# A third written order for 4871 operations of one attention and MLP kernel

## The chip, the cores and the metric

The kernel runs on one core of a Trainium2 chip, as one program. Its time is the device time in microseconds (us), the median of three runs. Besides the times there is one profiled execution of the kernel before, taken by the hardware profiler, with every instruction's start and duration. The engines are named as the profile names them: PE is TensorE, DVE is VectorE, ACT is ScalarE, POOL is GpSimd, and SP is the engine that issues most of the DMAs.

## The reference

```
scale = 1 / sqrt(64);  q, k, v: (8 batches, 8 heads, 576, 64), q and k drawn 8 times larger than v
k_p, v_p = k, v averaged over groups of 8 positions          # 576 -> 72 keys
scores = scale * q @ k_p^T;  scores -= max(scores)
attn = exp(scores) / (sum(exp(scores)) + 1e-09)
x = (attn @ v_p), heads side by side                        # (4608 tokens, 512)
h = x @ w_in                                                # 512 -> 2048
g = h * 1 / (1 + exp(-1.702 * h))
out = g @ w_out                                             # 2048 -> 512, float32
```

## The kernel before

**Attention.** Each of the eight batches goes through the same steps. Two heads' keys at a time are put on the partitions; scores go to PSUM tiles `sps` (L1148, PE), DVE takes the row maximum `nm` from each (L1171) and subtracts it into `sc` (L1179), ACT takes the exponential (L1200), DVE the sum (L1205). The weights are then copied into `main` and `tail` (L1271, L1262), turned by DVE (`mt`, L1378; `tt`, L1320) and cut into a high and a low part (`ah`, `al`, L1385, L1389; `at`, L1341, L1344). PE multiplies them with the values into `pav` (L1406 to L1409). Three instructions read each `pav`: `x` (L1448, its high part), `xt` (L1460, a copy) and the low part (L1451, always DVE). The `sps` and `pav` tiles share two PSUM banks, so a `pav` two further on can begin only when the last of the three reads of its bank is done.

**The MLP.** The tokens go through it in nine chunks: chunks 0 to 7 are the first 512 tokens of each batch, chunk 8 the 8 times 64 left over. Chunks 0 and 1 multiply in the plain way, three matmuls for each product of high and low parts (L1693 to L1695 into `h`, L1735 to L1737 into `o`). While chunk 1 runs, sums of weight blocks are made (`fold`: L1774, L1818, L1756, L1759, L437 and L440) and written to DRAM. Chunks 2 to 8 use a scheme of the Strassen kind with these sums: PE makes products in `ha` and `hb` (L1982), ACT or DVE copies them out (L1997), DVE adds (L2005), ACT takes the activation (L2017), the result is cut in two parts (L437 or L440, L2043, L2048, L2051) and goes into the output products (L2272 to L2274). `ha` and `hb` have two PSUM banks, the outputs four.

**The start.** SP issues loads of raw weights (`raw`, 512 KB each, L1555), of keys and values (`kv`, L622, 256 KB; `tl`, L683) and of queries (L2162). While these are on their way PE does idle matmuls (`warm`, L2225), and the first batch's attention runs before chunk 0.

**What sets the order.** The program first makes 4339 tasks, each with its engine, its instruction and the tiles that it reads and writes. Many tasks can run on a second engine (copies: ACT or DVE; subtractions and sums of SBUF tiles: DVE or POOL). Nothing is sorted when the program is built: the tasks are emitted as the table `ORDER` (L42) lists them, and each engine works off its own instructions in that order. A negative entry means the task's other engine:

```
    with tc.manual_schedule():
        for n in map(int, ORDER.split()):
            t = tasks[n if n >= 0 else -n - 1]
            if n < 0:
                t.swap()
            t.emit()
```

An instruction that waits therefore holds up everything behind it on its engine. Tile names in the lists below carry a batch or half, a piece, and the number of the tile's making.

Of the kernel before, what the change touches and what calls it, by code (L numbers as in the profile page):

```python
# [42 lines left out]
2074 2075 2076 2077 9 155 156 157 10 162 163 164 165 158 2078 2079 2080 2081 2082 73 0 2083 2084 2085 2086 2087 2088  # L43
2089 11 -161 169 170 171 4 6 3 31 1 5 22 159 72 166 172 173 32 25 26 33 7 8 50 2090 2 197 198 45 34 46 167 199 -52 52
23 24 212 47 35 213 36 214 48 49 215 53 21 190 191 192 54 2091 2092 29 12 30 176 177 37 40 41 42 2093 38 39 178 43 44
17 14 13 16 15 18 20 19 183 184 57 55 185 65 200 161 216 168 179 193 186 201 174 68 204 236 220 228 244 417 340 356
348 268 308 260 252 415 284 388 459 292 276 451 175 180 187 181 182 28 56 58 59 60 62 63 64 61 70 67 69 66 -196 -189
74 97 75 76 98 87 102 88 99 205 103 206 100 101 89 82 237 83 -91 207 91 112 104 77 84 189 113 105 -79 106 202 238 194
239 196 208 203 85 92 86 79 107 93 229 230 108 -81 -211 -219 231 81 114 94 117 95 115 109 96 110 111 116 217 221 222
209 223 119 118 120 121 124 123 240 232 2094 2095 2096 2097 2098 2099 2100 2101 2102 2103 219 224 211 226 233 2109  # L50
2110 2111 2112 2113 2114 2115 2116 -2105 136 -138 122 130 245 2117 246 2107 127 128 2105 2106 -132 -2119 247 253 254
261 262 -130 125 126 132 255 456 457 449 2119 133 300 324 416 418 -136 269 263 270 248 227 332 134 -235 235 2108 148
2120 2122 138 249 309 310 149 225 271 -142 -251 311 -140 140 2124 2125 2126 2127 142 2128 2129 2130 2131 277 278 241
-252 279 -144 2132 -2134 -243 -2135 2121 2123 264 256 312 285 286 287 144 150 2135 2137 301 302 27 -148 303 -152 357
145 266 152 146 -154 358 2218 2219 2220 2221 2222 2223 2224 2225 359 257 280 243 267 272 293 294 258 265 419 295 -260
2138 2226 -2228 421 422 -2229 2139 2140 2136 296 2141 2142 2143 2144 2145 2146 2229 2231 2232 282 341 342 343 281 274
349 350 420 -284 351 2147 2148 389 390 448 450 380 452 391 -2150 2233 2234 2235 2236 2237 2238 2239 2240 446 325 326
298 2241 425 426 327 458 154 404 2230 297 460 396 316 317 364 275 -2243 -2244 -300 372 428 427 2150 453 2154 2155 2156
2157 2244 2245 2158 2246 454 2247 304 360 318 273 319 352 288 365 289 366 313 344 320 328 392 429 430 71 424 367 455
333 -315 334 518 467 515 464 433 517 434 516 466 461 -291 462 2159 2160 2161 2162 2163 335 -316 -292 -2165 -307 373  # L60
374 375 519 2151 431 2152 393 305 2248 2249 2250 2251 2252 2253 2153 2254 2255 330 432 329 -308 465 -332 468 463 381
2256 -2258 605 472 604 475 474 525 473 523 524 526 382 322 368 376 336 2165 2166 2169 2170 469 2171 2172 2173 2174
2175 2167 2168 2258 2261 2176 435 346 321 383 345 337 405 361 406 470 476 471 407 423 323 436 347 2177 477 438 439
2178 338 437 -363 527 478 479 353 480 363 339 2259 2184 2185 2186 2187 2188 2189 2263 2190 2191 2260 2264 2265 2266
2267 2268 2269 2270 2262 440 -2180 441 442 2182 2180 481 482 485 484 378 2271 2272 483 354 397 398 -380 -2274 520 521
522 399 2183 528 529 530 2181 539 603 588 533 541 355 2192 540 542 486 589 400 -371 447 532 369 -2194 534 2278 606 444
2276 531 2279 503 2280 2281 -505 487 535 505 445 2194 377 489 490 543 488 371 2199 2200 401 394 2282 2201 491 2277 492
493 506 2197 -508 508 -396 536 537 538 384 385 -387 387 2283 2284 402 2274 544 545 546 494 2275 2285 2195 2286 2287
495 2202 509 -511 496 2203 2204 2196 497 2293 2294 2295 2296 2297 2198 2288 -499 511 499 512 2205 2206 2289 547 -404
2298 2299 2300 408 -411 636 637 639 409 513 2207 2208 411 548 549 514 550 552 551 607 590 2209 500 2291 2292 2308 553  # L70
2290 2214 2215 2309 2310 501 2301 554 613 612 643 592 610 591 2302 556 443 502 557 555 587 2311 2323 2324 558 565 2312
559 566 560 567 2210 2303 2325 2304 593 594 638 568 2326 2327 608 -598 -572 561 -563 640 2313 2314 2315 654 620 611
641 619 651 644 642 2211 -565 569 2316 -2318 412 563 -599 2328 2306 2307 2318 609 570 2329 2330 2342 572 579 -581 2305
2321 2343 2212 2216 573 574 581 2331 595 2332 575 578 600 614 -603 2526 2530 582 583 596 576 601 -600 -2334 577 616
-586 645 2353 2354 584 615 621 2319 2344 2355 2345 413 2320 2356 2322 617 2338 659 2357 2358 2359 414 2339 625 658 624
618 652 656 2546 2334 646 2335 623 2340 2531 2346 2527 2347 657 653 -2551 622 -2538 649 -2539 655 647 660 -2540 2543
648 650 2536 2336 2348 2375 2376 2377 2364 2378 2365 661 2366 2351 2367 2349 2350 2352 634 2551 2547 2368 2548 626 662
2544 2369 2370 -2558 2558 2549 628 664 -2541 -2542 635 728 2542 2559 2566 2545 2363 663 2552 627 665 586 727 2361 629
666 630 2362 -2557 2560 631 667 668 729 730 731 669 -2562 -674 -2571 847 2554 735 -690 2386 2372 2360 2371 2379 2380
685 2563 682 2381 2387 2388 2373 2389 2397 2398 2399 2400 2374 832 744 691 688 2532 675 686 2390 670 2391 2392 2385  # L80
2383 2382 2384 2408 2409 2394 2395 2410 2411 2571 732 -2565 -2554 2565 733 2562 734 -633 -694 2567 2568 2401 692 2528
-2687 -2578 -2579 -678 -685 -2530 -691 -2580 671 2402 2572 676 678 679 680 2687 2688 683 2583 2403 2419 2420 2393 2405
2396 2404 2421 2422 2407 2406 -2577 -2581 -2582 736 674 681 2412 2413 687 -673 -2703 -2534 -2591 2584 2414 -2707 2423
2424 2707 2430 694 697 695 2591 2582 742 2555 831 748 737 740 698 -2587 -2574 2694 696 2690 747 2418 2703 750 749 743
745 2416 2431 2441 2432 2433 706 2417 2415 2585 2425 2597 2587 2704 2434 707 2691 2695 751 746 738 739 741 -2607 -2597
2600 2435 2607 2608 2588 -634 708 -2719 2598 2599 2603 2436 2442 752 753 755 754 756 2428 2429 2426 2443 2444 2439
2427 2437 2452 2453 2440 2438 -2699 -2590 -2611 -2605 -2612 -2617 -2570 -2610 -2690 -2602 757 2605 2602 2612 2445 2446
2447 2617 758 759 760 -762 2696 -2627 2454 2463 2455 2456 2457 2451 2450 2464 2465 2466 2448 2449 2458 2474 2475 2460
2461 2462 699 -2619 -2631 -2620 2699 762 2627 2620 780 2467 -2622 2631 -2638 -775 779 2468 2592 -2723 -2637 -2594
-2639 -2640 768 2692 767 2632 2623 2628 2723 2640 2469 2459 2476 2485 2477 2486 2471 2487 2488 2472 2473 2470 2622  # L90
-2625 -2647 -2642 -2630 2643 -2645 885 700 2647 2478 701 879 2614 2534 2575 2594 2625 881 849 773 2479 2648 2480 713
-2651 2489 2651 2490 -2650 -2715 -2711 -2658 2777 -2634 2750 2642 2645 -2671 -2667 -2614 2654 887 882 -2659 2634 2574
2635 886 2595 2751 2535 2507 2508 2496 2497 709 2481 702 2498 2499 -715 715 -2660 720 -722 -785 722 -2720 -2668 770
771 777 765 781 2715 778 769 763 710 766 775 705 2668 783 785 -704 -713 704 -2670 786 787 -777 -783 711 2491 2693 2483
2484 2482 2509 2510 2492 833 2500 2671 2672 2501 772 2502 716 723 2494 2493 2495 2506 2503 2754 2504 788 726 764 2511
2512 789 2673 796 -798 798 -2677 719 724 2711 717 790 725 718 799 791 2652 2724 801 800 2700 792 793 795 2513 2615 884
2776 2774 2752 880 2753 2775 846 848 2674 2675 835 834 2505 2520 794 -2678 802 -804 804 805 808 810 -812 812 -820 813
2656 2523 2778 2514 2517 823 2755 -817 -821 -822 -828 -829 825 814 2779 -823 2521 829 -827 -825 2783 2757 2784 2515
2791 2792 -2759 2764 830 2796 2765 2798 -818 850 815 851 888 2734 2678 2679 836 2767 2705 2756 2759 806 807 2766 2760
# [2477 lines left out]
```

## Time and profile before

| | |
|---|---|
| median of three runs | 910.27 us (908.38 to 912.41) |
| profiled execution | 908.89 us, span of its instructions 907.0 us |
| PE busy | 855.6 us (94%) |
| DVE busy | 749.7 us (83%) |
| ACT busy | 571.5 us (63%) |
| POOL busy | 321.9 us (35%) |
| mean granted clock of PE | 0.990 |
| chain that ended last | PE 42%, DVE 31%, ACT 12%, DMA 6%, issue 5% |

The span runs from the first to the last instruction; the execution's own time is 1.89 us longer. The chain is followed back from the last instruction, at each step to what released it or to the instruction before it on its engine. Its shares are of the whole span, and stages with different limits are mixed in them. Granted clock is PE's clock as a share of full speed (2.4 GHz); 0.5 is the lower level of 1.2 GHz.

### The profile page before, as it was taken

To read this page: it belongs to the slowest core of one execution; us is meant where nothing else is said; L and a number is where in the kernel's file an instruction comes from. 1 tells how busy PE (TensorE), PEld (TensorE's weight loads), DVE (VectorE), ACT (ScalarE), POOL (GpSimd) and SP (SyncE) were. 2 spreads that over 40 slices of the span, in tenths; PEclk is the share of its full clock that TensorE was granted. 3 is DMA by queue.
4 is the path that set the end of the run, shared out by engine and by line. 5 is a ranking of instruction groups with operands and counts; after the bars stand their busy time and mean duration, and the time that the engine had idled before them with its cause. 6 is when DMAs were issued, how large, how long until landed. Compare 5 with 4: busy or idle time off the path is not lost.

```text
span 907.0 us, 16076 instructions
## 1 busy us (share of the span) xinstructions
PE 855.6 (94%) x5614; PEld 637.9 (70%) x5614; DVE 749.7 (83%) x1571; ACT 571.5 (63%) x1202; POOL 321.9 (35%) x307
## 2 busy tenths in 40 slices
PE   7999999998889888998999899999999999999997
PEld 7879888887666565666666566666667666666885
DVE  6999988879889979998687988999988666555787
ACT  6998853687678777777356645666476654424652
POOL 3765542552226453352332124122142224322122
PEclk9999999999989999999999999999999999999999
DMA  9974303320727653564447333643452155344542
GB/s 286 375 229 125 84 18 97 106 81 31 224 80 210 167 145 87 138 174 115 120 132 200 104 111 95 181 135 96 132 154 89 53 166 181 113 151 137 195 152 59
DMA packets 151313, 125.32 MB, mean 138 GB/s; under 512 B 86336, under 2 KB 108352, under 8 KB 151232
## 3 DMA queue, kind: packets, MB, share of 16 engines
q1 hardware_dynamic: 146384, 115.52, 43.5%
q10 hardware_dynamic: 4848, 8.78, 2.8%
q8 instruction: 44, 0.72, 0.3%
q14 instruction: 37, 0.30, 0.1%
HBM read 102.76 MB, written 21.50 MB: 137 GB/s over the span
## 4 chain that ended last, share of the span: by engine, by line
PE 42%; DVE 31%; ACT 12%; DMA 6%; issue 5%; SPq 3%; POOL 1%; ACTq 0%; DVEq 0%; POOLq 0%
PE ha L1982 9%; PE hb L1982 6%; PE o L2272 4%; PE o L2274 4%; PE o L2273 4%; ACT main L1271 3%; PE sps L1148 2%; ACT slots L2017 2%; DMA raw<-in_moe_w_in_dram 2%; DMA ws<-wd 1%; DVE slots L2005 1%; PE o_P L2502 1%; DVE nm L1171 1%; DVE qt L1132 1%; DVE sc L1179 1%
## 5 line engine op out<-in xcount | busy, mean ns | idle before, releaser
L1982 PEld LDWEIGHTS <-ws 128*128 128x128 f16 x2016 | 195.1, 98 | 81.7 <-issue 24.3
L1982 PE MATMUL ha<-x,ws 128*128 128x256 f16 x1008 | 137.6, 272 | 13.7 <-ACT slots L1997 3.6
L1982 PE MATMUL hb<-x,ws 128*128 128x256 f16 x1008 | 132.4, 273 | 5.5 <-DVE slots L2005 3.7
L2274 PE MATMUL o<-t,glall 128*128 128x512 f16 x256 | 97.0, 379 | 0.1
L2272 PE MATMUL o<-t,ghall 128*128 128x512 f16 x256 | 97.1, 379 | 0.0
L2273 PE MATMUL o<-t,ghall 128*128 128x512 f16 x256 | 97.0, 379 | 0.0
L1997 ACT COPY slots<-ha 128x256 f32<-128x256 f32 x94 | 34.7, 369 | 88.6 <-PE ha L1982 86.4
L2005 DVE TENSOR_TENSOR slots<-slots,hb 128x256 f32<-128x256 f32 x139 | 56.4, 410 | 34.8 <-PE hb L1982 24.3
L2017 ACT ACTIVATE slots<-slots,smalls 128x256 f32<-128x256 f32 (+1 forms) x108 | 61.4, 577 | 34.8 <-DVE slots L2005 33.5
L1693 PE MATMUL h<-x,w 128*128 128x256 f32 (+1 forms) x192 | 63.2, 329 | 1.0 <-ACT g L1710 0.6
L1271 ACT COPY main<-sc 32x384 f32<-32x384 f32 (+2 forms) x117 | 53.0, 453 | 15.5 <-DVE mt L1378 6.1
L1723 POOL TENSOR_TENSOR gl<-g,gh 128x512 fp32r<-128x512 f32 x23 | 31.0, 1347 | 87.0 <-ACT gh L1715 60.8
L1695 PE MATMUL h<-x,w 128*128 128x256 f32 (+1 forms) x192 | 61.2, 319 | 0.0
L1694 PE MATMUL h<-x,w 128*128 128x256 f32 (+1 forms) x192 | 61.1, 318 | 0.0
L2048 POOL TENSOR_TENSOR slots<-slots,smalls 128x512 f32<-128x512 f32 (+1 forms) x32 | 33.6, 1050 | 61.2 <-ACT ghall L437 20.2
L1148 PE MATMUL sps<-k,qt 128*128 128x144 f32 x320 | 49.2, 299 | 5.7 <-DVE sc L1179 2.5
L1389 POOL TENSOR_TENSOR al<-mt,ah 128x256 fp32r<-128x256 f32 (+1 forms) x20 | 17.6, 882 | 98.4 <-ACT ah L1385 39.8
L1148 PEld LDWEIGHTS sps<-k,qt 128*128 128x128 f32 x320 | 44.9, 198 | 9.4 <-issue 3.3
L2274 PE MATMUL o<-t,slots 128*128 128x512 f16 x128 | 48.5, 379 | 1.6 <-DVE slots L2043 1.6
L2272 PE MATMUL o<-t,slots 128*128 128x512 f16 x128 | 48.6, 379 | 0.0
L2273 PE MATMUL o<-t,slots 128*128 128x512 f16 x128 | 48.5, 379 | 0.0
L1982 PE MATMUL ha<-x,shared 128*128 128x256 f16 x336 | 46.3, 275 | 2.3 <-ACT slots L1997 1.1
(399 smaller groups left out, 2269.6 us busy)
## 6 DMA issues: line engine op xcount, KB each, us to landing
ws<-wd SPq DMA_DIRECT2D x168, 256.0 KB
out_dram<-osb ACTq DMA_DIRECT2D x32, 256.0 KB
raw<-in_moe_w_in_dram SPq DMA_DIRECT2D x15, 512.0 KB
raw<-in_moe_w_out_dram SPq DMA_DIRECT2D x15, 512.0 KB
kv_False<-in_k_dram SPq DMA_DIRECT2D x28, 256.0 KB
kv_True<-in_v_dram SPq DMA_DIRECT2D x28, 256.0 KB
shared<-wd SPq DMA_DIRECT2D x56, 128.0 KB
qr<-in_q_dram SPq DMA_DIRECT2D x112, 40.0 KB
```

What stands on the lines that cost most here:

```text
L1148: nc.tensor.matmul(ps()[:, t * PW : (t + 1) * PW], lhsT=qt()[:, s0 : s0 + P], rhs=m.k2()[:, jj], start=True, stop=True,)
L1271: copy(out=main()[32 * r : 32 * (r + 1), :, cols].rearrange("p j t (k a) -> p t j a k", a=2), in_=sc()[rows, ts, :, 16 * r : 16 * (r + 1)] ...
L1693: nc.tensor.matmul(o, lhsT=w[:, 0, j], rhs=xs[:, 0], start=j == 0, stop=False)
L1694: nc.tensor.matmul(o, lhsT=w[:, 1, j], rhs=xs[:, 0], start=False, stop=False)
L1695: nc.tensor.matmul(o, lhsT=w[:, 0, j], rhs=xs[:, 1], start=False, stop=j == NJ - 1)
L1982: nc.tensor.matmul(o, lhsT=wv()[:, r, jj], rhs=xo(k, jj), start=start and n == 0, stop=n == len(terms) - 1,  skip_group_check=not start,)
L1997: t = copy(256, lambda copy: copy(out=part(i), in_=bank()[:, 0:256]), [bank], [at(i)])
L2005: lambda: nc.vector.tensor_tensor(out=part(i), in0=part(i), in1=hb()[:, half * 256 : half * 256 + 256], op=ALU.add),
L2017: lambda: nc.scalar.activation(out=out(), in_=src(), func=AF.Gelu_apprx_sigmoid, scale=inner()),
L2272: nc.tensor.matmul(o(), lhsT=gh()[:, tok], rhs=wp[:, 0], start=start, stop=False)
L2273: nc.tensor.matmul(o(), lhsT=gh()[:, tok], rhs=wp[:, 1], start=False, stop=False)
L2274: nc.tensor.matmul(o(), lhsT=gl()[:, tok], rhs=wp[:, 0], start=False, stop=stop)
```

## The change

Only the table `ORDER` differs: the same 4339 tasks, in another order, and with another choice of engine for some. It has 4871 entries; one stands on average 29 places from where it stood (median 19, at most 373). Negative entries go from 709 to 711. By the lists of instructions, PE has 9177 on both sides and SP 693; DVE has 1571 before and 1555 after, ACT 1174 and 1164 (30 table loads on both), POOL 307 and 334. What moved to POOL is mostly `gl` (L1723, 23 to 29), `al` (L1389, 20 to 23), `at` (L1344, 12 to 16), the low parts L1759 (39 to 41), L2072 (23 to 28), L1818 (10 to 13) and the weighting L1221 (1 to 3). ACT gives and takes L437 (DVE's form is L440: 76 to 65) and L1756 (DVE 13 to 25).

The beginning of the table, before and after:

```diff
 ORDER = """
-2074 2075 2076 2077 9 155 156 157 10 162 163 164 165 158 2078 2079 2080 2081 2082 73 0 2083 2084 2085 2086 2087 2088
...
+2074 72 9 155 156 2075 2076 2077 2078 2079 2080 2081 2082 2083 2084 2085 2 1 157 6 0 5 25 26 23 24 158 160 161 73 3 4
...
```

**DVE at the scores of the third batch's second half**, in the second plain chunk. `sps_1_0` and `sps_1_1` are the first two pieces, in the two banks; `nm` is the maximum and `sc` the subtraction, which frees the bank. Before:

```order
L1171 TENSOR_REDUCE nm_1_2414<-sps_1_1_2410 128x3x2
L1344 TENSOR_TENSOR at_0_1_2392<-tt_0_2390,at_0_1_2392 32x256
L1774 TENSOR_TENSOR stage<-w_6_753 128x512
L1759 TENSOR_TENSOR t_5_2286<-t_5_2286 128x256
L1344 TENSOR_TENSOR at_0_0_2395<-tt_0_2390,at_0_0_2395 32x256
L1378 STREAM_TRANSPOSE mt_0_1_2449<-main_0_2179 128x256
L1132 STREAM_TRANSPOSE qt_1_3_2472<-qr_1_3_2404 128x320
L1132 STREAM_TRANSPOSE qt_1_2_2474<-qr_1_2_2241 128x320
L1171 TENSOR_REDUCE nm_1_2414<-sps_1_0_2406 128x3x2
L1179 TENSOR_TENSOR sc_1_2477<-sps_1_0_2406,nm_1_2414 128x3x144
L1179 TENSOR_TENSOR sc_1_2477<-sps_1_1_2410,nm_1_2414 128x3x144
```

After:

```order
L1171 TENSOR_REDUCE nm_1_2430<-sps_1_1_2379 128x3x2
L1774 TENSOR_TENSOR shared_2432<-w_0_358 128x512
L1132 STREAM_TRANSPOSE qt_1_3_2434<-qr_1_3_2311 128x320
L1171 TENSOR_REDUCE nm_1_2430<-sps_1_0_2375 128x3x2
L1179 TENSOR_TENSOR sc_1_2437<-sps_1_0_2375,nm_1_2430 128x3x144
L1132 STREAM_TRANSPOSE qt_1_2_2439<-qr_1_2_2300 128x320
L1179 TENSOR_TENSOR sc_1_2437<-sps_1_1_2379,nm_1_2430 128x3x144
```

Between the first maximum and the second there stood seven instructions (two `at`, a weight sum, its low part, a turn of `main`, two turns of queries); now two stand there, and one turn of queries comes between the two subtractions.

**ACT at the same batch's `pav`**, some 40 us later. `pav_0_0` and `pav_0_1` are the two tiles in the banks, and `x` and `xt` read them. Before:

```order
L1271 COPY main_1_2817<-sc_1_2477 32x3x4x2x16 x4
L1271 COPY main_1_2817<-sc_1_2477 32x4x2x16
L437 ACTIVATE t_7_2830<-shared_2419,smalls 128x512
L1271 COPY main_1_2817<-sc_1_2477 32x3x4x2x16 x3
L1448 CAST x_2835<-pav_0_1_2789 128x256
L1271 COPY main_1_2817<-sc_1_2477 32x3x4x2x16 x2
L1460 COPY xt_0_2839<-pav_0_0_2797 128x256
```

After:

```order
L1448 CAST x_2782<-pav_0_0_2761 128x256
L1756 CAST t_12_2778<-t_12_2778 128x512
L1460 COPY xt_0_2785<-pav_0_0_2761 128x256
L1271 COPY main_1_2835<-sc_1_2437 32x3x4x2x16 x6
L1271 COPY main_1_2835<-sc_1_2437 32x4x2x16
L1271 COPY main_1_2835<-sc_1_2437 32x3x4x2x16
L1710 ACTIVATE g_0_14_2887<-h_0_14_2755 128x512
L437 ACTIVATE t_14_2889<-stage,smalls 128x512
L1715 ACTIVATE gh_0_14_2891<-h_0_14_2755 128x512
L1460 COPY xt_0_2785<-pav_0_1_2799 128x256
```

Before, ten copies to `main` and an L437 stand ahead of the last of these reads; now both reads of `pav_0_0` come ahead of the copies, and the read of `pav_0_1` behind eight of them, two activations and an L437. (x4 and the like: so many alike in a row.)

**ACT at the products of chunk 2's seventh hidden part** (`ha_6`), where the next batch's `pav` also falls. Before:

```order
L1997 COPY slots_3247<-ha_6_3755 128x256
L1341 CAST at_0_1_3777<-tt_0_3768 32x256 x2
L1448 CAST x_3797<-pav_0_1_3792 128x256
L1460 COPY xt_0_3826<-pav_0_1_3792 128x256
L437 ACTIVATE slots_3403<-slots_3056,smalls 128x512
L1997 COPY slots_3045<-ha_6_3755 128x256
L2017 ACTIVATE gall<-gall,smalls 128x256
L1997 COPY slots_3247<-ha_6_3755 128x256
```

After:

```order
L1997 COPY slots_3261<-ha_6_3788 128x256
L1385 CAST ah_0_0_3828<-mt_0_0_3824 128x256
L1997 COPY slots_3065<-ha_6_3788 128x256
L916 COPY k_1887<-kbd_3597 32x4x32 x3
L1997 COPY slots_3261<-ha_6_3788 128x256
L916 COPY k_1887<-kbd_3597 32x4x32 x4
L2017 ACTIVATE slots_3261<-slots_3261,smalls 128x256
L2017 ACTIVATE slots_3261<-ha_6_3788,smalls 128x256
L1200 ACT_TABLE_LOAD
L1200 ACTIVATE sc_1_3768<-sc_1_3768 128x1728
L437 ACTIVATE ghall<-slots_3261,smalls 128x512
L1460 COPY xt_0_3948<-pav_0_0_3890 128x256
L1997 COPY slots_3065<-ha_7_3950 128x256
```

The two reads of a `pav` stood between two copies out of `ha_6`; now `ah`, seven copies of keys and the third copy stand there, and the first `pav` read comes after the table load and exponential that follow.

On SP, the loads before were raw w_in, raw w_out, raw w_in, kv, tl, kv, kv, tl, raw w_in, two of queries, and only then the last kv of the first batch's keys; now they are raw w_in, kv, kv, tl, tl, kv, kv, and then raw w_out, raw w_in and queries. Two raw loads, 1.0 MB, have moved behind the keys.

## Rows read from the trace of the kernel before

**Rows 1.** Windows: stretch, length, busy time (x count) by engine, granted clock, DMA share, GB/s.
```profile
0.00:39.00 39.00, 34.26 (x229) 30.97 (x229) 29.43 (x67) 29.05 (x61) 20.22 (x24) 0.96 0.98 323
39.00:200.00 161.00, 158.43 (x938) 137.82 (x938) 138.87 (x265) 117.48 (x239) 79.44 (x66) 1.00 0.41 119
200.00:425.00 225.00, 200.71 (x1218) 146.13 (x1217) 205.68 (x405) 172.20 (x356) 88.48 (x80) 0.97 0.47 134
425.00:580.00 155.00, 148.26 (x996) 100.37 (x994) 128.30 (x281) 83.24 (x176) 44.33 (x42) 1.00 0.48 132
580.00:900.00 320.00, 312.36 (x2236) 222.10 (x2235) 244.71 (x553) 169.49 (x372) 89.44 (x99) 1.00 0.43 131
```

**Rows 2.** Waits of the matmul engine: waited for, us in total, times, longest us.
```profile
PE pav L1406 <- DVE x L1451: 6.0, 2, 4.8
...
PE sps L1148 <- DVE sc L1179: 2.5, 1, 2.5
```

**Rows 3.** Timeline of VectorE, 199 to 207 us: start, us, engine, line, operation [idle before].
```profile
198.94 1.18 DVE L1344 TENSOR_TENSOR at<-tt,at 32x256 fp32r<-32x256 f32 x1 [0.65 <-ACT at L1341]
200.15 1.67 DVE L1774 TENSOR_TENSOR stage<-w 128x512 f32<-128x512 f32 x1
...
205.60 1.12 DVE L1179 TENSOR_TENSOR sc<-sps,nm 128x432 f32<-128x432 f32 x2
206.64 0.68 DVE L1774 TENSOR_TENSOR stage<-w 128x512 f32<-128x512 f32 x1
```

**Rows 4.** Timeline of TensorE, 206 to 209 us.
```profile
206.36 2.72 PE L1148 MATMUL sps<-k,qt 128*128 128x144 f32 x12 [2.54 <-DVE sc L1179]
...
209.31 0.63 PE L1736 MATMUL o<-w,gh 128*128 128x512 f32 x1
```

**Rows 5.** Timeline of VectorE, 250 us.
```profile
249.97 0.42 DVE L1448 CAST x<-pav 128x256 f16<-128x256 f32 x1 [4.14 <-ACT xt L1460]
```

**Rows 6.** Timeline of ScalarE, 243 to 250 us.
```profile
243.55 2.50 ACT L1271 COPY main<-sc 32x384 f32<-32x384 f32 x5 [6.10 <-DVE mt L1378]
...
249.59 0.35 ACT L1460 COPY xt<-pav 128x256 f32<-128x256 f32 x1
```

**Rows 7.** Timeline of TensorE, 251 to 259 us.
```profile
251.11 0.48 PE L1406 MATMUL pav<-ah,vh 128*128 128x256 f32 x1 [4.77 <-DVE x L1451]
...
253.45 0.58 PE L1406 MATMUL pav<-ah,vh 128*128 128x256 f32 x1 [1.21 <-DVE x L1451]
...
254.47 0.63 PE L1735 MATMUL o<-w,gh 128*128 128x512 f32 x1
...
258.21 0.39 PE L1735 MATMUL o<-w,gh 128*128 128x512 f32 x1
```

**Rows 8.** Timeline of ScalarE, 327 to 328 us.
```profile
327.11 0.37 ACT L1460 COPY xt<-pav 128x256 f32<-128x256 f32 x1 [3.07 <-DVE x L1451]
...
328.14 0.35 ACT L1997 COPY slots<-ha 128x256 f32<-128x256 f32 x1
```

**Rows 9.** Timeline of TensorE, 328 us.
```profile
328.54 0.81 PE L1982 MATMUL ha<-x,ws 128*128 128x256 f16 x6 [2.38 <-ACT slots L1997]
```

**Rows 10.** Windows around the third stall.
```profile
330.00:340.00 10.00, 10.00 (x58) 6.83 (x57) 7.50 (x17) 9.14 (x17) 3.66 (x4) 0.84 0.42 117
```

**Rows 11.** Timeline of the SP queue, 11 us: issue of a load of keys.
```profile
11.48 1.68 SPq L622 DMA_DIRECT2D kv<-in_k_dram  x1
```

**Rows 12.** Timeline of TensorE, 21 us.
```profile
21.16 0.76 PE L1148 MATMUL sps<-k,qt 128*128 128x144 f32 x4 [1.94 <-ACT k L1052]
```

**Rows 13.** Timeline of GpSimd, 200 us.
```profile
199.80 1.47 POOL L1723 TENSOR_TENSOR gl<-g,gh 128x512 fp32r<-128x512 f32 x1
```

**Rows 14.** Groups by line and form on VectorE: busy us, mean ns, idle before.
```profile
L1774 DVE TENSOR_TENSOR stage<-w 128x512 f32<-128x512 f32 x12 | 10.0, 841 | 0.1
```

**Rows 15.** The same groups on GpSimd.
```profile
L1723 POOL TENSOR_TENSOR gl<-g,gh 128x512 fp32r<-128x512 f32 x23 | 31.0, 1347 | 87.0 <-ACT gh L1715 60.8 <-ACT k L936 10.3 <-DVE smalls L804 8.4
...
L1389 POOL TENSOR_TENSOR al<-mt,ah 128x256 fp32r<-128x256 f32 x13 | 11.6, 892 | 65.0 <-DVE ah L1385 24.4 <-ACT ah L1385 20.3 <-ACT slots L2017 20.3
```

408 rows, old and new, of the table ORDER are left out of this document.

## The prediction

> **What bounds the kernel now.** I read the windows by stage first, since the page's shares are averages. PE is busy 94% of the span, so the time is PE's work plus the gaps in it, and a change of order can only touch the gaps (and the stretches at a lower granted clock behind them). The windows [rows 1] show where they lie. PE's idle time is the length less its busy time: 4.7 us before 39 us, 2.6 in 39 to 200, 24.3 in 200 to 425, 6.7 in 425 to 580 and 7.6 in 580 to 900, some 46 us. The granted clock is 1.00 from 39 to 200 us and from 425 on, 0.97 in 200 to 425 and 0.96 at the start. So more than half of what an order can win stands in 200 to 425 us, the second plain chunk and the first two of the Strassen kind. In the same stretch DVE is busy 205.7 of 225 us (91%), against 83% and 76% in the two behind it: DVE is the engine that is nearly full there, and what stands ahead of a needed instruction on it decides the gaps.
>
> Second, PE's waits [rows 2]: the largest sum is 6.0 us in two waits for the last read of a `pav`; a single wait of 2.5 us is for the subtraction that frees a score bank. Third, the timelines at the longest waits, and beside them the same places in the written order, before and after. Three places in 200 to 425 us and the start carry the sum.
>
> **The change part by part.** *Place one, scores.* DVE's turn to the subtraction came late: seven instructions ran from 198.94 us, and the two subtractions began at 205.60 [rows 3]. PE's third piece waited 2.54 us for them, and the matmuls behind it ran at a lower clock, 0.63 us each at 209.31 [rows 4] where the same one takes 0.39 later [rows 7]. In the new order two instructions stand between the two maxima: a weight sum of 0.68 us (alone) or 1.67 (beside POOL) [rows 3] and a turn of queries of about half a us. The subtraction would then begin some 3.5 to 4.5 us earlier, which is more than 2.54. So the stall goes. With it goes the slow clock: matmuls that start 0.42 us apart in place of 0.23 (from the first `o` matmul shown in [rows 7] to the last, nine in 3.74 us where nine at 0.23 take 2.1) lost 0.18 each; six of them and the scores make about 1.2. Term: -3.7. The bounds are -4.5 (the work pushed aside finds free time) and 0 (a weight sum that now comes later holds up something else).
>
> *Place two, `pav`.* ACT ran copies to `main` from 243.55 and read `xt` only at 249.59 [rows 6]; DVE's read of the same bank sat idle 4.14 us until then [rows 5]; PE waited 4.77 and 1.21 us behind it, then ran nine matmuls at the slow spacing [rows 7]: 1.6 us, and 0.7 more on the eight `pav` matmuls. That is 8.3 us lost. Now both ACT reads of `pav_0_0` stand ahead of the copies; DVE's last read follows with one instruction of the weights in front. The read of `pav_0_1` still stands behind eight copies (0.5 us each by [rows 6], 2.50 for five), two activations and an L437, some 6 us of ACT, and then twelve DVE instructions; between those two `pav` and their successors PE has about as much other work (28 matmuls in the order). So I take the first wait as gone and up to 2 us left at the second: -6. Bounds: -8.3 and -1 (the wait only moves to `pav_0_1`).
>
> *Place three, `ha_6`.* ACT's `xt` read waited 3.07 us for DVE, and the copy out of `ha_6` stood behind it at 328.14 [rows 8]; PE waited 2.38 [rows 9] and had a clock of 0.84 in the ten us from 330, in which it was busy throughout [rows 10]: 16% of 10 is 1.6 more, 4.0 in all. The new order has no `pav` read between those copies; seven key copies stand there instead. But the `pav` reads now come behind a table load and an exponential, so some of the wait can return there. I take -3, bounds -4.0 and +1.
>
> *The start.* Two raw loads, 1.0 MB, move behind the first keys; the last of them is issued at 11.48 us [rows 11] and will be issued before the queries. At 323 GB/s in this stretch [rows 1] 1.0 MB is 3.1 us. Only part of it counts: PE waits 1.94 us for keys at 21.16 [rows 12], and the weights that come later are needed at 39 us. I take -2; bounds -5 (both that wait and the transfer time) and +1 (weights late for the first chunk).
>
> *The engine choice.* DVE loses 16 instructions. At 0.6 us, between a 256-wide one and the 0.84 of a 512-wide one [rows 14], that is 9.7 us. POOL gains 27, between 0.89 and 1.35 us each [rows 15], 24.5 by their forms. POOL is busy 35%, so its own time is covered. But DVE pays for it: its 512-wide weight sum took 1.67 us at 200.15 while POOL was busy from 199.80 [rows 13], and 0.68 at 206.64 [rows 3]. That is 1.0 us lost in one meeting. Taking a fifth of DVE's time as of that kind (two SBUF inputs: subtractions, sums and low parts, by the groups by form), 24.5 us of POOL meets about 5 us of it. DVE is then 5 us freer, not 10, most of it behind 580 us where PE is idle 7.6 of 320. I count +2 for meetings in the full stretch. The bounds are -3 (the relief shows in full) and +15 (every us of POOL meets such a DVE instruction: 24.5 less 9.7).
>
> The Trainium skill, page "SBUF — State Buffer", section "Who interferes with whom", says that a DVE instruction with two SBUF inputs and a GpSimd instruction that reads SBUF exclude each other for a whole instruction, whichever starts first. The row at 200.15 agrees, with 1.0 us lost. By that rule alone the change would tend to the upper bound, since nearly all that moved is of this kind; it is the second rival below.
>
> *What else moves.* Adding up, at the mean of each form, the instructions that stand ahead of the same matmul on each engine, the new order has 4.5 to 6.5 us more of DVE ahead in chunk 4 (about 465 to 510 us), and 4 to 11 us less of DVE and 3 to 10 less of ACT behind 580. In chunk 4 PE idles little now (6.7 of 155 us), so part of those 5.5 us may become new waits: +4, bounds 0 and +6.5. Small new waits elsewhere, since every entry moved by 29 places on average: +2, bounds -3 and +6, the size of the two stretches' gaps.
>
> *The sum.* -3.7 - 6 - 3 - 2 + 2 + 4 + 2 = -6.7. The profiled execution took 908.9, so 902.2; the median of the runs shown is 1.4 above it, so 903.5 us as a median.
>
> **The rivals.** *The gaps only move (no change).* DVE is 91% full in 200 to 425 and the order changes nothing in the sum there; each gap removed lets PE run ahead until the next DVE instruction is late. For it: place two's second `pav` and the `ha_6` reads, which each have a new late read. Against it: DVE's own idle time there was 19 us, and 4.14 of it came from ACT's late read at 250 us [rows 5], which a better order gives back. Then 13 of the 14.7 us return and about -1.7 is left: some 908.5.
>
> *The shared path of POOL and DVE (slower).* The place is every stretch where POOL's added 24.5 us runs beside a two-input DVE instruction. It is worth 1.0 us per meeting [rows 3, 13], and it decides from the point where over 40% of the added POOL time meets one (9.7 of 24.5): then DVE is fuller than before. At the whole 24.5 DVE has +15; with half of that on the path in 200 to 580 us, and the gaps moved as in the first rival: 910.3 + 7 = 917. Against it: POOL is idle 65%, and most of the added POOL work lies behind 580 us, where DVE is 76% busy.
>
> *The large gain.* If the new order treats all late reads as it does these three, half of the 24.3 us of gaps in 200 to 425 and of the 0.03 of clock there (6.8 us) goes, -15.5, with -2 at the start and -2 behind 580: about 890. For it: the three places checked all improve, and they are the three longest. Against it: the remaining gaps are short ones with many releasers.
>
> **How the numbers follow.** A measurement of this kernel tells 0.5%, about 4.5 us, from no change. Chances: the forecast 0.42, from 897 to 906; large gain 0.14, near 890; no change 0.27, 905.7 to 914.8; slower 0.17, about 917. Faster by over 0.5% (below 905.7) is the forecast and the large gain, 0.56; within 0.27; slower 0.17. The range takes in the large gain down to 889 and the slower case's near edge at 916, leaving about 0.2 out.
>
> **What would show it.** Place one right: PE's third score piece of the third batch has no wait over 0.5 us, and no clock under 0.9 there. Place two: the largest `pav` wait under 2 us, and DVE's `x` read not idle behind ACT. Place three: no wait over 1 us at `ha_6`. Start: the first `h` matmul before 38 us. Chunk 4 wrong: PE idle above 11 us in the 155 us behind 425. The shared path: DVE's busy time down by less than 5 us although it has 16 fewer instructions; above 750 the rival is at work. The forecast is wrong if PE's idle time in the plain and first Strassen chunks stays above 20 us, or if the time is over 908.

## The result, and the profile after

The new order took 869.45 us (median of 4 runs, 867.37 to 870.41) against 911.34 us for the kernel before (908.38 to 912.99): a ratio of 0.9541, interval 0.9509 to 0.9573. It is faster, as forecast, but by six times the forecast: 41.9 us where 6.7 were expected, and outside the range of 889 to 916. The profiled executions stand at 908.89 and 869.25 us; the difference of 39.6 us is what is followed here. One figure above is wrong: the table names 4871 different tasks, not 4339. A comparison of the two tables task by task also shows more than the counts of instructions did: 716 tasks run on another engine, 253 moved from ACT to DVE, 243 from DVE to ACT, 123 from DVE to POOL and 97 back.

The head of the page after: busy time and share of the span by engine, the chain by engine.

```profile
PE 841.3 (97%) x5614; PEld 632.2 (73%) x5614; DVE 728.3 (84%) x1555; ACT 566.6 (65%) x1192; POOL 345.9 (40%) x334
...
PE 74%; DVE 11%; ACT 6%; DMA 4%; issue 2%; SPq 2%; POOL 0%; ACTq 0%; DVEq 0%; POOLq 0%
```

PE's busy time fell by 14.3 us for the same 5614 matmuls, and its idle time from 51.4 us (907.0 less 855.6) to 26.2. The granted clock, now 1.000 in place of 0.990, accounts for some 9 us of the first (0.010 of 855.6): before, it stood at 1.2 GHz for 17 us in all, in four places that each follow one of the long waits (from 22.6, 206.9, 251.3 and 329.8 us). The other 5 us or so come with the gaps. In an unbroken row a 128x512 matmul is shown for 0.39 us and the next one starts 0.23 after it (at 235.26, 235.49 and 235.73 in the new kernel), but ahead of a gap it counts in full. PE has 43 gaps in place of 69; 26 times 0.16 us is about 4, an estimate. DVE's busy time fell by 21.4 us, POOL's rose by 24.0. The chain is now PE in 74% of the span, where it was in 42%: for three quarters of the time PE's own work sets the end.

The windows after, in the columns of [rows 1] (the last stretch ends at 860):

```profile
0.00:39.00 39.00, 32.51 (x228) 28.91 (x228) 29.52 (x69) 26.34 (x57) 17.56 (x21) 1.00 0.95 305
39.00:200.00 161.00, 156.94 (x936) 137.67 (x935) 141.11 (x272) 114.15 (x231) 86.65 (x76) 1.00 0.42 121
200.00:425.00 225.00, 215.91 (x1362) 156.74 (x1361) 214.23 (x442) 177.16 (x371) 94.71 (x83) 1.00 0.52 150
425.00:580.00 155.00, 154.86 (x1071) 108.03 (x1069) 131.07 (x293) 98.04 (x200) 58.92 (x57) 1.00 0.50 141
580.00:860.00 280.00, 278.17 (x2015) 199.69 (x2014) 209.30 (x479) 150.93 (x335) 88.06 (x100) 1.00 0.43 133
```

In 425 to 580 us PE is idle 0.14 us where it was idle 6.7, and behind that 1.8 in 280 us where it was 7.6 in 320. In 200 to 425 it is idle 9.1 in place of 24.3, and the clock is 1.00 in all five. At the start and in 39 to 200 us no idle time was won (6.5 and 4.1 us; 4.7 and 2.6 before). The same stretch of time holds other work before and after, so the table of the experiments cuts by chunk.

PE's waits after, which answer to [rows 2] (waited for: us in total, times, longest):

```profile
PE hb L1982 <- DVE slots L2005: 2.7, 5, 0.9
PE ha L1982 <- ACT gall L1997: 2.2, 1, 2.2
PE h L1693 <- ACT gh L1715: 1.7, 1, 1.7
PE pav L1406 <- DVE sc L1179: 1.7, 2, 1.0
```

The 6.0 us for the last read of a `pav` and the 2.5 us for the score subtraction are gone, and no wait is over 2.2 us.

At the scores, DVE, which answers to [rows 3], and PE, which answers to [rows 4]:

```profile
197.18 0.59 DVE L1171 TENSOR_REDUCE nm<-sps 128x6 f32<-128x432 f32 x1
197.69 0.68 DVE L1774 TENSOR_TENSOR shared<-w 128x512 f32<-128x512 f32 x1
...
199.32 0.61 DVE L1179 TENSOR_TENSOR sc<-sps,nm 128x432 f32<-128x432 f32 x1
```

```profile
201.79 1.63 PE L1148 MATMUL sps<-k,qt 128*128 128x144 f32 x12
```

From the first maximum to the first subtraction it is 2.1 us. PE's third piece came without a wait, and its twelve matmuls took 1.63 us where they had taken 2.72.

At the same batch's `pav`: ACT, which answers to [rows 6], DVE to [rows 5], PE to [rows 7].

```profile
234.64 0.35 ACT L1448 CAST x<-pav 128x256 f16<-128x256 f32 x1
...
235.42 0.37 ACT L1460 COPY xt<-pav 128x256 f32<-128x256 f32 x1
235.81 4.13 ACT L1271 COPY main<-sc 32x384 f32<-32x384 f32 x8
...
241.69 0.36 ACT L1460 COPY xt<-pav 128x256 f32<-128x256 f32 x1
```

```profile
236.03 0.41 DVE L1451 TENSOR_TENSOR x<-pav,x 128x256 f16<-128x256 f32 x1
...
242.29 0.42 DVE L1448 CAST x<-pav 128x256 f16<-128x256 f32 x1
242.74 0.42 DVE L1451 TENSOR_TENSOR x<-pav,x 128x256 f16<-128x256 f32 x1
```

```profile
236.99 0.28 PE L1409 MATMUL pav<-al,vh 128*128 128x256 f32 x1
...
242.66 0.28 PE L1406 MATMUL pav<-ah,vh 128*128 128x256 f32 x1
...
243.22 0.38 PE L1406 MATMUL pav<-ah,vh 128*128 128x256 f32 x1
```

ACT's second `xt` read still comes late, at 241.69, 4.4 us after its `pav` was written (236.99 and 0.28). Nobody waits: PE has other work until 242.66, and the `pav` that needs this bank begins at 243.22, when DVE's last read (242.74 and 0.42) has just ended.

At `ha_6`, ACT, which answers to [rows 8], and PE, which answers to [rows 9]:

```profile
314.70 0.36 ACT L1997 COPY slots<-ha 128x256 f32<-128x256 f32 x1
...
316.05 0.36 ACT L1997 COPY slots<-ha 128x256 f32<-128x256 f32 x1
```

```profile
315.11 0.81 PE L1982 MATMUL ha<-x,ws 128*128 128x256 f16 x6
...
317.94 0.36 PE L1406 MATMUL pav<-ah,vh 128*128 128x256 f32 x1 [0.70 <-DVE sc L1179]
```

The copies out of `ha_6` stand on time and PE has no wait there; the `pav` behind them waits 0.70 us.

The start, SP, which answers to [rows 11], and PE, to [rows 12]:

```profile
1.26 1.32 SPq L622 DMA_DIRECT2D kv<-in_k_dram  x2
...
3.98 1.28 SPq L622 DMA_DIRECT2D kv<-in_k_dram  x2
```

```profile
15.52 0.66 PE L1120 MATMUL qps<-ident,q 128*128 128x128 f32 x4 [0.88 <-DMA q<-in_q_dram]
...
21.91 2.02 PE L725 MATMUL red_v<-kv,ident 128*128 128x128 f32 x16 [1.29 <-DMA kv<-in_v_dram]
...
39.03 0.37 PE L1693 MATMUL h<-x,w 128*128 128x256 f32 x1
```

The last load of keys is issued by 5.3 us in place of 11.48, and the wait of 1.94 us for keys is gone. In its place PE waits for queries (0.88) and for values (1.29), and the first `h` matmul comes at 39.03 us; it had come at 38.98.

### The profile page after: what moved, and what is told of

Read it like the earlier page. It is cut to its first block, busy times and chain, and to the rows that moved or that the text cites. A ratio compares the mean times of both kernels' runs of the same rounds, so it can differ in the third digit from the quotient of the medians.

```text
span 867.5 us, 16062 instructions
## 1 busy us (share of the span) xinstructions
PE 841.3 (97%) x5614; PEld 632.2 (73%) x5614; DVE 728.3 (84%) x1555; ACT 566.6 (65%) x1192; POOL 345.9 (40%) x334
## 4 chain that ended last, share of the span: by engine, by line
PE 74%; DVE 11%; ACT 6%; DMA 4%; issue 2%; SPq 2%; POOL 0%; ACTq 0%; DVEq 0%; POOLq 0%
PE ha L1982 14%; PE hb L1982 10%; PE o L2272 8%; PE o L2273 8%; PE o L2274 8%; PE sps L1148 3%; PE h L1693 3%; PE h L1695 2%; PE h L1694 2%; PE o L1736 2%; PE o L1735 2%; PE o L1737 2%; PE o_P L2502 2%; PE bankZ L2502 1%; DMA shared<-wd 1%
## 5 line engine op out<-in xcount | busy, mean ns | idle before, releaser
L1997 ACT COPY slots<-ha 128x256 f32<-128x256 f32 x95 | 34.9, 369 | 78.8 <-PE ha L1982 77.9
L2005 DVE TENSOR_TENSOR slots<-slots,hb 128x256 f32<-128x256 f32 x139 | 56.1, 412 | 27.4 <-PE hb L1982 18.8
L1723 POOL TENSOR_TENSOR gl<-g,gh 128x512 fp32r<-128x512 f32 x29 | 41.2, 1419 | 68.8 <-ACT gh L1715 57.0
L1271 ACT COPY main<-sc 32x256 f32<-32x256 f32 (+2 forms) x113 | 51.3, 454 | 4.2 <-DVE sc L1221 1.3
L1344 POOL TENSOR_TENSOR at<-tt,at 32x320 fp32r<-32x320 f32 (+1 forms) x16 | 14.1, 879 | 92.4 <-ACT at L1341 67.1
L2048 POOL TENSOR_TENSOR slots<-slots,smalls 128x512 f32<-128x512 f32 (+1 forms) x32 | 31.4, 980 | 47.7 <-DVE ghall L440 21.1
L1389 POOL TENSOR_TENSOR al<-mt,ah 128x256 fp32r<-128x256 f32 (+1 forms) x23 | 18.9, 824 | 75.8 <-ACT ah L1385 41.3
L1148 PE MATMUL sps<-k,qt 128*128 128x144 f32 x320 | 46.3, 288 | 2.4 <-ACT qt L1127 1.4
L2274 PEld LDWEIGHTS <-glall 128*128 128x128 f16 x256 | 25.1, 98 | 30.2
```

Source lines behind the costliest of these rows:

```text
L1148: nc.tensor.matmul(ps()[:, t * PW : (t + 1) * PW], lhsT=qt()[:, s0 : s0 + P], rhs=m.k2()[:, jj], start=True, stop=True,)
L1271: copy(out=main()[32 * r : 32 * (r + 1), :, cols].rearrange("p j t (k a) -> p t j a k", a=2), in_=sc()[rows, ts, :, 16 * r : 16 * (r + 1)] ...
L1723: engine.tensor_tensor(out=gl(), in0=g(), in1=gh().bitcast(F32), op=ALU.subtract)
L2005: lambda: nc.vector.tensor_tensor(out=part(i), in0=part(i), in1=hb()[:, half * 256 : half * 256 + 256], op=ALU.add),
L2274: nc.tensor.matmul(o(), lhsT=gl()[:, tok], rhs=wp[:, 0], start=False, stop=stop)
```

## The experiments

Theory A: the order is what counts (no engine stands behind a late instruction any more). Theory B: it is the choice of engine. Theory C: the two only fit together. Theory D: the early part gives the later chunks a lead. The ratios compare each run with the kernel before on the same chip, where its median was 908.3 to 911.9 us. PE's idle time is the length of a stretch less PE's busy time, from windows cut at the first product of chunks 2, 3 and 8; the first stretch begins at the first `h` matmul.

| run | time, us | ratio to before (interval) | idle to chunk 2 | chunk 2 | chunks 3 to 7 |
|---|---|---|---|---|---|
| before | 911.34 | | 11.5 | 11.3 | 18.2 |
| after | 869.45 | 0.9541 (0.9509 to 0.9573) | 4.1 | 9.0 | 1.4 |
| e1, new order, old choice | 978.42 | 1.0719 (1.0676 to 1.0763) | 14.2 | 26.0 | 42.2 |
| e2, old order, new choice | 998.52 | 1.0951 (1.0911 to 1.0991) | 30.4 | 24.5 | 50.3 |
| e3, new to chunk 2, then old | 906.68 | 0.9945 (0.9913 to 0.9976) | 4.0 | 17.2 | 19.6 |
| e4, old to chunk 2, then new | 886.87 | 0.9711 (0.9677 to 0.9746) | 11.8 | 11.8 | 2.1 |
| e5, new, ACT/DVE choices old | 944.55 | 1.0353 (1.0305 to 1.0400) | 13.6 | 18.6 | 27.1 |
| e6, new, DVE/POOL choices old | 928.25 | 1.0177 (1.0130 to 1.0225) | 7.6 | 21.2 | 23.2 |
| e7, old, three places repaired | 907.37 | 0.9959 (0.9918 to 1.0001) | 12.9 | 9.0 | 19.7 |
| e8, new, a tenth of the choices old | 879.32 | 0.9635 (0.9590 to 0.9679) | 6.5 | 10.6 | 4.2 |
| e9, new, ACT and DVE shifted | 914.64 | 1.0034 (1.0016 to 1.0052) | 4.1 | 8.9 | 28.8 |
| e10, new, PE shifted | 903.86 | 0.9918 (0.9892 to 0.9943) | 5.0 | 8.9 | 19.5 |
| e11, new, one old fault put back | 875.12 | 0.9611 (0.9585 to 0.9638) | 8.6 | 7.8 | 1.3 |
| e12, old, ACT and DVE shifted | 938.62 | 1.0326 (1.0276 to 1.0377) | 13.4 | 12.2 | 35.4 |

**Order or choice (e1, e2).**

```diff
 # e1: the new table, each entry with the engine that it has in the old one; e2 the other way round
-ORDER = new
+ORDER = [n if swapped_old[task(n)] == (n < 0) else -n - 1 for n in new]
```

> The new order with the old choice of engine for all 716 tasks whose engine differs between the two tables. Theory A (the gain is the order: no engine stands behind a late instruction any more): 868 to 882 us. Theory B (the gain is the choice, work taken from DVE and ACT to POOL): 900 to 912. Theory C (order and choice only fit together; with other engines the rows ahead of a needed read differ): 885 to 910, with waits of PE of 1 to 4 us at new places.

> The old order with the new choice of engine. Theory A: 905 to 915 us, PE idle about 50. Theory B: 870 to 885. Theory C: 900 to 925, no better than before.

A and B both fall as the whole explanation. Either half alone makes the kernel slower than before, by 7% and 10%, and PE's idle time grows in every stretch. C holds, well beyond its numbers: e1 has the same counts of instructions on each engine as the kernel before and still loses 67 us to it.

**Stage by stage (e3, e4).**

```diff
-ORDER = new
+ORDER = new[:1388] + [n for n in old if task(n) not in tasks(new[:1388])]   # e3; e4: old[:1387], then new
```

> The new table (order and choice) up to the first Strassen product of chunk 2, then the rest in the old order and choice. From the two traces PE's lost time (its starts less its work at full speed) up to that product is 23.2 us before and 10.4 after. If gains stay in their stage (theory A): 911 less 13, 896 to 901. If the early part also gives the later chunks their lead (theory D): 875 to 890.

> The old table up to the first Strassen product of chunk 2, then the rest in the new order and choice. If gains stay in their stage (theory A): 911 less 27, 881 to 887. If the later gain needs the early part's lead (theory D): 895 to 910.

The window of chunks 3 to 7 in the kernel before, and in the new one:

```profile
360.80:812.80 452.00, 433.80 (x2925) 294.81 (x2924) 367.39 (x803) 257.90 (x543) 135.99 (x131) 1.00 0.46 131
```

```profile
349.80:774.30 424.50, 423.11 (x2897) 291.37 (x2895) 347.68 (x775) 256.38 (x537) 140.75 (x137) 1.00 0.47 136
```

The same chunks in e4, and in e3:

```profile
366.20:791.20 425.00, 422.92 (x2895) 291.21 (x2893) 349.20 (x775) 256.22 (x537) 140.40 (x137) 1.00 0.47 136
```

```profile
355.00:808.80 453.80, 434.19 (x2927) 294.66 (x2925) 367.21 (x803) 257.24 (x541) 135.47 (x132) 1.00 0.47 131
```

PE's idle time in chunks 3 to 7 goes with the table of these chunks (2.1 and 19.6; 1.4 and 18.2 in the whole kernels), and the idle time up to chunk 2 with the table of that part. So D falls: no lead is handed on. e4 came out as A's sum said. e3 missed it by some 6 us: at the seam chunk 2 has 17.2 us idle, one wait for `pav` of 6.5 among them, more than either whole kernel. The two halves together bring 29 of the 42 us; most of the rest is lost at e3's seam, where chunk 2 took 108.7 us for 600 matmuls (101.2 for 598 in the kernel before).

**Repairing the three places alone (e7).** Nothing else moved in ACT's list but six tasks by one to four places, and nothing on PE.

```diff
 # DVE, before the second maximum of the third batch's second half
-L1344 at, L1774, L1759, L1344 at, L1378 mt, L1132, L1132, L1171 nm, L1179 sc, L1179 sc
+L1132, L1132, L1171 nm, L1179 sc, L1179 sc, L1344 at, L1774, L1759, L1344 at, L1378 mt
 # ACT, pav2_0
-L1271 main x8, L437 among them, L1448 x<-pav2_0_1, L1271 x2, L1460 xt<-pav2_0_0
+L1448 x<-pav2_0_1, L1460 xt<-pav2_0_0, L1271 main x10, L437 among them
 # ACT, ha2_6
-L1448 x<-pav3_0_1, L1460 xt<-pav3_0_1, L437, L1997 slots<-ha2_6
+L437, L1997 slots<-ha2_6, L1448 x<-pav3_0_1, L1460 xt<-pav3_0_1
```

> The kernel before, its own order and choices, with three places repaired: five DVE instructions moved behind the two score subtractions of the third batch's second half, ACT's two reads of pav2_0 moved ahead of the copies to main, and the two copies and L437 of the ha_6 place put the other way round to the pav reads. By the prediction's terms: 3.7 + 8.3 + 3 less, so 896 to 899 us. If such gaps only move to the next late instruction (the first rival): 905 to 912.

The chain of it at `pav2_0`: ACT, DVE and PE of e7.

```profile
238.14 0.37 ACT L1448 CAST x<-pav 128x256 f16<-128x256 f32 x1 [2.22 <-PE pav L1409]
239.31 0.37 ACT L1460 COPY xt<-pav 128x256 f32<-128x256 f32 x1 [0.80 <-PE pav L1409]
...
245.26 2.65 ACT L1271 COPY main<-sc 32x384 f32<-32x384 f32 x5
247.93 0.62 ACT L1756 CAST t<-t 128x512 f16<-128x512 f32 x1
```

```profile
244.88 0.40 DVE L1451 TENSOR_TENSOR x<-pav,x 128x256 f16<-128x256 f32 x1
248.58 0.69 DVE L1759 TENSOR_TENSOR t<-t 128x512 f16<-128x512 f32 x1 [3.31 <-ACT t L1756]
...
250.67 0.42 DVE L1451 TENSOR_TENSOR x<-pav,x 128x256 f16<-128x256 f32 x1
```

```profile
245.33 0.39 PE L1406 MATMUL pav<-ah,vh 128*128 128x256 f32 x1 [0.54 <-DVE x L1451]
...
251.15 0.58 PE L1406 MATMUL pav<-ah,vh 128*128 128x256 f32 x1 [5.08 <-DVE x L1451]
```

ACT reads both `pav` some 10 us earlier than before, and PE's first wait shrinks from 4.77 to 0.54 us. But DVE's next instruction, L1759, waits 3.31 us for L1756, which ACT reaches only behind its copies at 247.93; DVE's read of the other `pav` stands behind it, at 250.67; and PE waits 5.08 us at the next `pav`, where it had waited 1.21. Place two has 5.6 us of waits where it had 6.0. The score stall is gone too, and 2.21 us at 215 us (for L1715 on ACT) stand in its place. At `ha_6` the 2.38 us did not come back, but two waits behind it grew by 1.6 to 1.7 us each (1.56 to 3.25 at 342 us, 1.39 to 3.02 at 501); no run says whether the repairs did that. Repairs worth 15 us by their stalls brought some 4 us, and the interval (0.9918 to 1.0001) does not exclude that they brought nothing. Here the first rival was right, at two places of three: in the old order a gap moves on to the next late instruction.

**How the misfits add up (e5, e6, e8).**

```diff
-ORDER = new
+ORDER = new with 496 (e5: ACT/DVE), 220 (e6: DVE/POOL) or a random 72 (e8) of the 716 choices as in old
```

> The new order; of the 716 differing choices of engine only the 496 between ACT and DVE (copies and scalings) are set back to the old ones. With all 716 set back it took 978 us, 109 more than the new kernel. If the costs of misfits add up one by one (theory C1, 0.15 us each): 945 us. If a few spoil the order and the rest adds little (C2): 960 to 985. If the choices between DVE and POOL are what counts (C3, length and shared path): 870 to 900.

> The new order; only the 220 choices between DVE and POOL are set back to the old ones. C1: 903 us. C2: 920 to 970. C3: 940 to 980.

> The new order; a random tenth (72) of the 716 differing choices is set back to the old ones. C1: 880 us. C2: 895 to 940. If a misfit is mostly absorbed by free time (C4): within 3 us of 869.

e5 and e8 fall on C1: 75 us for 496 is 0.15 us each, 10 us for 72 (47 between ACT and DVE, 25 between DVE and POOL) is 0.14, and 109 for all 716 is 0.15. e6 does not: 59 us for 220, 0.27 each. Nor do the two parts add up: 75 and 59 make 134, more than the 109 for both at once. So the price of a misfit is an average over many and depends on the others. A part of e6's loss shows on its page:

```profile
PE 859.0 (93%) x5614; PEld 636.8 (69%) x5614; DVE 768.7 (83%) x1581; ACT 567.1 (61%) x1192; POOL 323.1 (35%) x307
```

DVE has 26 instructions more than in the new kernel and is busy 40.4 us longer; at 0.6 us each 26 make 16. The other 25 us are longer instructions. In e6's trace 104 DVE instructions run over 0.2 us longer than the quickest tenth of their form, and all 104 overlap an instruction on POOL, as only 34% of all DVE instructions do; in the new kernel there are 75, all of them so. So DVE and POOL do get in each other's way where the choices do not fit the order. How much of the 59 us that makes, no run shows. In e5 it is something else: its DVE is busy 732.5 us, nearly as in the new kernel (728.3), and PE is idle 27.1 us in chunks 3 to 7 all the same.

**Is the order exact (e9, e10, e12)?**

```diff
-list of an engine, from the first product of chunk 3 on
+the same list sorted by (place + random 0..3): e9 new, ACT and DVE; e10 new, PE; e12 old, ACT and DVE
```

> The new kernel; from the first product of chunk 3 on 255 ACT and 355 DVE tasks stand one or two places from where they stood, in each engine's own list; choices of engine, and PE's list but for three tasks, as they are. Theory T (the gain of chunks 3 to 8 hangs on the exact rows of ACT and DVE): 0.03 us or more for each, 885 to 900 us, PE losing 15 to 30 us more there. Theory L (small shifts are absorbed, and the gain lies in larger moves or in the choices): 868 to 873.

> The new kernel; from chunk 3 on 330 of PE's 778 tasks (groups of matmuls) stand one or two places from where they stood, the other engines' lists as they are. If what counts is which ready work PE has in front of a late result (theory P): 885 to 905 us. If PE's order is loose and the others' promptness counts (theory Q): 868 to 875.

> The kernel before, shifted in the same way as e9: from the first product of chunk 3 on 253 ACT and 394 DVE tasks stand one or two places off, PE's list and all choices as they are. The new kernel lost 44 us by such shifts. If the old order is as exactly fitted, only less well (theory T): 930 to 960 us. If it is already no better than a shifted one (theory U: the new order's gain is fit that the old one lacks): 908 to 920.

PE's waits of e9 from chunk 3 to 7, the longest groups:

```profile
PE hb L1982 <- DVE slots L2005: 5.0, 6, 2.6
PE ha L1982 <- DVE slots L1997: 4.7, 5, 1.7
PE o L2272 <- ACT osb L1653: 4.2, 1, 4.2
PE ha L1982 <- DVE slots L2005: 3.1, 4, 1.5
```

The same groups in the new kernel, from 350 to 774 us (one is left):

```profile
PE hb L1982 <- DVE slots L2005: 1.1, 2, 0.9
```

Theory T holds in e9, by more than it said, and theory P in e10. Shifts of one or two places take back the whole gain of 42 us (e9) or 34 us of it (e10), with the same instructions on the same engines, and DVE as busy as before the shift (730.8 us in all). The waits are again many and short, behind copies (L1997) and sums (L2005) that come a little late, as in the kernel before. Both kinds of list count: PE's, which says what it has to do meanwhile, and those of the engines that read its banks. In e12 the old order loses 27 to 30 us by such a shift (647 tasks; 610 in e9), less than the new one's 45: theory T again. By this measure the old table was fitted as well, less closely. Each of e8, e9, e10 and e12 is one random draw; how far another draw would differ was not measured.

**One fault put back (e11).**

```diff
 # ACT, pav2_0 of the new order
-L1448 x<-pav2_0_0, L1756, L1460 xt<-pav2_0_0, L1271 main x8
+L1756, L1271 main x8, L1448 x<-pav2_0_0, L1460 xt<-pav2_0_0
```

> The new kernel with one fault of the old one put back: ACT's two reads of pav2_0_0 stand behind the eight copies to main that followed them; nothing else moved. If that place is worth what the prediction took for it (8.3 us of stall and slow clock, less 2 of cover): 874 to 878 us, with a wait of PE for pav of 2 to 5 us near 243 us. If the new order has time to spare there: 868 to 871.

ACT, DVE and PE of e11:

```profile
235.38 4.09 ACT L1271 COPY main<-sc 32x384 f32<-32x384 f32 x8
239.47 0.37 ACT L1448 CAST x<-pav 128x256 f16<-128x256 f32 x1
```

```profile
240.16 0.42 DVE L1451 TENSOR_TENSOR x<-pav,x 128x256 f16<-128x256 f32 x1 [4.11 <-ACT xt L1460]
```

```profile
247.79 0.38 PE L1406 MATMUL pav<-ah,vh 128*128 128x256 f32 x1 [4.55 <-DVE x L1451]
```

The reads come 4 to 5 us later and PE waits 4.55 us, at the second `pav`, not at the one whose reads were moved: DVE stood idle 4.11 us for its read, and its whole list behind it is late. The price is 5.7 us of time (875.12 less 869.45), within what was expected. So this place costs about what its stall says when all around it fits (e11), and its repair brought next to nothing where the rows behind it are late as well (e7).

To take one engine's list alone from the other table was not tried, so how much of the gain belongs to each engine's list stays open. No run was faster than the new kernel.

## Why the prediction was wrong

- **Direction and places: right.** The three stalls are gone, with the slow clock behind each, and place two went wholly, not to 2 us. In 200 to 425 us PE's idle time fell by 15.2 us.
- **The three places as terms that add up (-3.7, -6, -3): about right in sum, wrong in kind.** With the start and the +2 they make -12.7, and chunk 2 ended 11.0 us earlier (349.8 us, 360.8 before) with 29 more matmuls done. The slow clock in place one was taken too small: the score matmuls alone gained 1.1 us (2.72 to 1.63), where 1.2 stood for them and six others at 0.18. But e7 shows that repairing the three in the old order gives about 4 us, not 15. They were worth their stalls only where the rows behind them fit too (e11, for place two). A sign of it stood in [rows 6] and was not used: ACT sat idle 6.10 us ahead of the copies, with `pav` reads behind them that it could have done (e7 does them in that time).
- **The start (-2): not seen.** The keys came earlier and PE waited for queries and values instead. The first `h` matmul came at 37.0 to 39.0 us in four executions with the old start (before, e4, e7, e12) and at 38.3 to 39.1 in five with the new one, so a term of that size is hard to tell from the spread, and none of it shows.
- **The shared path of DVE and POOL (+2): wrong in sign as far as DVE's busy time tells.** POOL got 24 us more, and DVE came down by 21.4, 9.7 by the count and the rest by shorter instructions. Nor does most of POOL's added work lie behind 580 us, as the second rival's argument had it: 15.7 of the 24.0 us come before chunk 3 (163.7 us to 179.4). In the groups by form, which answer to [rows 14] and [rows 15]:

```profile
L1774 DVE TENSOR_TENSOR stage<-w 128x512 f32<-128x512 f32 x14 | 11.1, 796 | 0.0
```

```profile
L1723 POOL TENSOR_TENSOR gl<-g,gh 128x512 fp32r<-128x512 f32 x29 | 41.2, 1419 | 68.8 <-ACT gh L1715 57.0 <-PE sps L1148 7.2 <-DVE gh L1719 4.3
...
L1389 POOL TENSOR_TENSOR al<-mt,ah 128x256 fp32r<-128x256 f32 x12 | 9.4, 786 | 52.4 <-ACT ah L1385 29.1 <-DVE ah L1385 9.0 <-PE sps L1148 6.9
```

The weight sum takes 796 ns on average in place of 841. The meetings are a matter of order: e2 has the same instructions on the same engines as the new kernel, in the old order, and its DVE is busy 755.5 us in place of 728.3. The Trainium skill, page "SBUF — State Buffer", section "Who interferes with whom", puts it as "Issue order, not op shape, decides who blocks". The trace agrees so far as those 27 us go; which instruction held the path at each meeting was not followed. The second rival (slower, 917) is out for this change.
- **The step that failed: "What else moves" (+4 in chunk 4, +2 elsewhere).** It weighed how much work stands ahead on each engine and let the remaining short waits stand, with new ones added. In chunks 3 to 7 they went from 18.2 us of idle time to 1.4. These chunks took 424.5 us in place of 452.0, with 28 fewer of the 2925 matmuls in them (some 4 us at 0.146 each); in 425 to 580 us, where the +4 stood, PE is idle 0.14 us. Less work on DVE was not enough for it: e5 has the lighter DVE and 27.1 us idle. By the waits of e9 and e10, what counts at each bank that is handed over is whether the reader stands at the right place among its neighbours, and whether PE has work until then. Sums of the work ahead don't show that: shifts of a place or two leave them nearly as they are, and cost 34 to 45 us.
- **The large gain (890, 0.14) was the right rival and too small.** It took half of one stretch's gaps and clock. Measured were 25.2 us of gaps over the whole span and 14.3 of PE's busy time, some 9 of them clock.
- **The rule of what would show it wrong** named PE idle over 20 us in the middle and a time over 908, both on the slow side; nothing was named for a miss on the fast side.

What stays open: by what rule the new table was made. The runs show that the gain lies in order and choice together, stage by stage, and that small shifts undo it. They do not show which of its rows each microsecond hangs on.

## What to carry to other kernels

When a written order is replaced as a whole, its possible gain is all of the bound engine's idle time and slow clock (here 51 us and some 9), and the range should reach there; the longest stalls don't measure it. A stall that is repaired alone can come back at the next late instruction (here at two places of three), so judge an order by its short waits, stage by stage. Order and choice of engine are one thing: change one engine's list, or some choices, and the rest has to be fitted again.

## What the runs showed that was not expected

A shift of 610 tasks by one or two places costs 45 us, 0.07 us each. A misfit in the choice of engine costs 0.15 us between ACT and DVE (496 of them), 0.27 between DVE and POOL (220) and 0.14 in a mixed tenth (72), and less together than apart. The same instructions keep DVE busy 728.3 us in one order and 755.5 in another (e2). In both shifted versions of the new kernel (e9, e10) one wait of 4.2 to 4.4 us for an output copy on ACT (L1653) appeared that neither whole kernel has among its longest waits.
